# Clustered attention and SwiGLU on one core: q, k and x transposed off TensorE in the later part

## The chip, the core and the metric

The kernel runs on one core of a Trainium2 chip. A core has a matrix engine (TensorE, PE in the profile; its weight loads are PEld), VectorE (DVE), ScalarE (ACT), GpSimd (POOL), a queue engine that issues transfers (SyncE, SP) and 16 DMA engines. The engines run side by side, each through its own list of instructions in order, and wait for one another by semaphores. The metric is the time of one execution on the device, in microseconds (us); less is better.

## The reference

Inputs are float32: q, k, v of 4 batches x 8 heads x 768 tokens x 64, 16 centroids per head, and the weights of a feed-forward layer. The output is 3072 x 512 float32.

```python
def _attn_ref(q, k, v, centroids):              # q, k, v: (4, 8, 768, 64)
    ...
    q_assign = np.argmax(np.einsum('bhsd,hcd->bhsc', q_n, c_n), axis=-1)
    k_assign = np.argmax(np.einsum('bhsd,hcd->bhsc', k_n, c_n), axis=-1)
    mask = q_assign[:, :, :, None] == k_assign[:, :, None, :]
    scores = scale * np.matmul(q, k.transpose(0, 1, 3, 2))
    scores = np.where(mask, scores, -1000000000.0)
    ...                                         # softmax over the keys
    return np.matmul(attn, v)

def _moe_ref(x, w_gate, w_val, w_out, rms_g):   # x: (3072, 512), d_ff 1536
    rms = np.sqrt(np.mean(x * x, axis=-1, keepdims=True) + 1e-06)
    xn = x / rms * rms_g
    g = xn @ w_gate
    silu = g * (1.0 / (1.0 + np.exp(-g)))
    return silu * (xn @ w_val) @ w_out
```

A query attends only to the keys of its own cluster. The heads of a token, side by side, are the rows x of the second part.

## The kernel before

The work is cut in eight units (a batch, and half of its queries: 384 tokens by 8 heads; u = 0 to 7 in the code) and eight groups of four heads (g = 0 to 7), in which q and k are prepared. Head n of 32 belongs to group n // 4. While TensorE computes the scores of unit u, the gaps are filled with the second part for units u - 1 and u - 2, and from u = 1 on with the preparation of group u + 2 (and of group 2 in unit 1).

Loads come in rows of six tokens per partition, and TensorE transposes q and k, 128 columns at a time, into PSUM. ACT moves them to `qkT`; GpSimd and VectorE cast them to bf16 into `qext` and `kext`.

```python
    def src(a, n):
        b, h = divmod(n, H)
        return a[b, h].rearrange("(p t) d -> p t d", t=ST)      # ST = 6

    def load(n, part, on=None):
        if n not in staged:
            staged[n] = stage.tile([P, 2, ST, D], F32, tag="qk", name="qk")   # 6 buffers
        (on or nc.sync).dma_start(out=staged[n][:, part], in_=src((q, k)[part], n))
    ...
    def trans(g, h, part, on=None):
        if (g, h // 2) not in qkT:
            qkT[g, h // 2] = qk32.tile([P, 2, 2, UQ], F32, tag="qkT", name="qkT")
        qk = staged[g * HG + h]
        ps = ps_g.tile([P, UQ], F32, tag="gen", name="tq")
        for i in range(HT):                                     # HT = 3
            nc.tensor.transpose(ps[:, i * P:(i + 1) * P], qk[:, part, 2 * i:2 * i + 2].rearrange("p t d -> p (t d)"),
                                ident_f)
        to, by = qkT[g, h // 2][:, h % 2, part], 1.0 / ZS if part else 1.0
        if on is nc.vector:
            nc.vector.tensor_scalar_mul(to, ps, by)
        else:
            nc.scalar.activation(to, ps, ACT.Copy, scale=by)
```

The centroids are multiplied with `qkT` (tile `sc`). VectorE makes one-hot rows of the largest products and transposes them (`oh`); `place` writes them by DMA into rows 64 to 79 of `qext` and `kext`. A score of two tokens of the same cluster so has a large constant added, which the exponential takes away again.

```python
    def place(on, g, m, es=(0, 1)):
        ext = (kext if m else qext)[g % 4]
        for h in range(HG):
            for e in es:
                on.dma_start(out=ext[D:D + NC, h, e * UQ:(e + 1) * UQ],
                             in_=put[g, m][32 * h + e * NC:32 * h + (e + 1) * NC])
```

Group 2 is placed from SyncE, later ones from GpSimd. The attention writes x (`pv`). Its squares are summed by ACT (by VectorE for units 0 and 1), VectorE normalizes, TensorE transposes, and VectorE evicts with the gain of the norm:

```python
    def rms(u):
        x, nt = xs[u], UNITS[u][2]
        for t in range(nt):
            squares(u, t, True)
        ...                                                     # y = 1 / rms, nine small VectorE instructions
        for t in range(nt):
            nc.vector.tensor_scalar_mul(xn[u][:, t], x[:, t], y[:, t:t + 1])

    def xtrans(u, c):
        if c == 0:
            xnT[u] = xp.tile([P, CC, UQ], BF16, tag="xnT", name="xnT")
        ps = ps_g.tile([P, UQ], BF16, tag="gen", name="tx")
        w = UNITS[u][2] * P
        for t in range(UNITS[u][2]):
            nc.tensor.transpose(ps[:, t * P:(t + 1) * P], xn[u][:, t, c * P:(c + 1) * P], ident)
        nc.vector.tensor_scalar_mul(xnT[u][:, c, :w], ps[:, :w], gcol[:, c:c + 1])
```

`gv(u, f, val)` multiplies `xnT` with a block of 128 columns of a weight (four matmuls, tile `gate` or `val`); `out_mm(u, t, part)` does a third of an output row block (four matmuls, tile `o`). In `attention`, after each piece of scores (`s`: two matmuls and one exponential by ACT) fill is issued in proportion to its listed cost:

```python
    for u in range(1, NU):
        ...
            fill = ffn_work(u - 2)[CUT:] + [(0.0, lambda u=u: rms(u - 1))]
            fill += ... border(o, ffn)              # o pieces of unit u - 2, xtrans of unit u - 1 among the last
            attention([(u, h) for h in range(H)], fill + spread(ffn[CC:CUT], group(g) if g < NG else []), 1 if g < NG else 0)
```

So a unit holds, in this order, the last 8 gate or val pieces of unit u - 2, the norm of u - 1, the 9 output pieces of u - 2 with the transposes of x, and 16 gate or val pieces of u - 1 with the preparation of a group. Head n + 6 of q and k, and head n + 8 of v, are loaded as head n is prepared.

Of the kernel before, what the change touches and what calls it, by code (L numbers as in the profile page):

```python
# [9 lines left out]
F32 = mybir.dt.float32  # L10
BF16 = mybir.dt.bfloat16
# [11 lines left out]
def kernel(  # L23
# [27 lines left out]
    scale = 1.0 / (D ** 0.5)  # L51
    KR = D + NC
    WARM = 7
    CUT = CC + 2 * FC - 8
    LEAD = 6
    NQ, NV = 6, 8

    ctx.enter_context(tc.manual_schedule())
    pool = lambda n, b, **kw: ctx.enter_context(tc.tile_pool(name=n, bufs=b, **kw))
# [16 lines left out]
    def src(a, n):  # L76
        b, h = divmod(n, H)
        return a[b, h].rearrange("(p t) d -> p t d", t=ST)

    def load(n, part, on=None):  # L80
        if n not in staged:
            staged[n] = stage.tile([P, 2, ST, D], F32, tag="qk", name="qk")
        (on or nc.sync).dma_start(out=staged[n][:, part], in_=src((q, k)[part], n))

    def load_qk(n):
        if n < B * H:
# [6 lines left out]
        stagedv[n] = stage.tile([P, ST, D], F32, tag="vs", name="vs", bufs=NV)  # L93
        (vq or nc.sync).dma_start(out=stagedv[n], in_=src(v, n))

    c_in = const.tile([P, D], F32)
    nc.sync.dma_start(out=c_in, in_=centroids.rearrange("h c d -> (h c) d"))
    load(0, 0)
    load(0, 1, nc.scalar)
# [2 lines left out]
    for n in range(2, NQ):  # L102
        load(n, 1)
        load(n, 0)
    gcol = const.tile([P, CC], F32)


    qext = [const.tile([P, HG, S], BF16, name=f"qext{i}") for i in range(4)]
# [30 lines left out]
        return y2  # L139


    ones = const.tile([P, 32], F32)
    nc.vector.memset(ones, 1.0)
    cnt = const.tile([P, 32], F32)
    nc.vector.tensor_tensor_scan(cnt, ones, ones, 0.0, op0=ALU.mult, op1=ALU.add)
    cntT = const.tile([P, 32], F32)
    nc.vector.transpose(cntT, cnt)
    ident_f = const.tile([P, P], F32)
    nc.vector.memset(ident_f, 0.0)
# [13 lines left out]

    cblk = const.tile([P, H, 2 * NC], F32)
    nc.gpsimd.memset(cblk, 0.0)
    c_sq = const.tile([P, D], F32)
# [9 lines left out]
    c_n = const.tile([P, 2 * D], F32)  # L176
    nc.vector.tensor_scalar_mul(c_n[:, :D], c_in, c_inv)
    nc.vector.tensor_scalar_mul(c_n[:, D:], c_in, c_inv)

# [22 lines left out]
    def trans(g, h, part, on=None):  # L202
        if (g, h // 2) not in qkT:
            qkT[g, h // 2] = qk32.tile([P, 2, 2, UQ], F32, tag="qkT", name="qkT")
        qk = staged[g * HG + h]
        ps = ps_g.tile([P, UQ], F32, tag="gen", name="tq")
        for i in range(HT):
            nc.tensor.transpose(ps[:, i * P:(i + 1) * P], qk[:, part, 2 * i:2 * i + 2].rearrange("p t d -> p (t d)"),  # L208
# [11 lines left out]
    def cast(on, g, h, part, es=(0, 1)):  # L220
        for e in es:
            to = cols((kext if part else qext)[g % 4][:D, h], g, e)
            of = qkT[g, h // 2][e * D:(e + 1) * D, h % 2, part]
            if on is nc.scalar:
                nc.scalar.copy(to, of)
            else:
                on.tensor_copy(to, of)  # L227
# [138 lines left out]
    def squares(u, t, last):  # L366
        if (t, last) == (0, False):
            sq[u] = small.tile([P, 2, HT], F32, tag="ss", name="ss")
            xn[u] = xp.tile([P, HT, DM], BF16, tag="xn", name="xn")
        c = slice(DM - 2 * D, DM) if last else slice(0, DM - 2 * D)  # L370
        to = sq[u][:, int(last), t:t + 1]
        if u <= 1:
            nc.vector.scalar_tensor_tensor(xn[u][:, t, c], xs[u][:, t, c], 1.0 / DM, xs[u][:, t, c], op0=ALU.mult,
                                           op1=ALU.mult, accum_out=to)
        else:
            nc.scalar.activation(xn[u][:, t, c], xs[u][:, t, c], ACT.Square, scale=DM ** -0.5, accum_out=to)  # L376
# [5 lines that stand above are left out]
        ms = small.tile([P, HT], F32, tag="ms", name="ms")  # L382
        nc.vector.scalar_tensor_tensor(ms[:, :nt], sq[u][:, 0, :nt], 1e-6, sq[u][:, 1, :nt], op0=ALU.add, op1=ALU.add)
        y = rsqrt(ms[:, :nt], nt)
        for t in range(nt):
            nc.vector.tensor_scalar_mul(xn[u][:, t], x[:, t], y[:, t:t + 1])

    xnT, gvT = {}, {}

# [4 lines that stand above are left out]
        w = UNITS[u][2] * P  # L394
        for t in range(UNITS[u][2]):
            nc.tensor.transpose(ps[:, t * P:(t + 1) * P], xn[u][:, t, c * P:(c + 1) * P], ident)  # L396
        nc.vector.tensor_scalar_mul(xnT[u][:, c, :w], ps[:, :w], gcol[:, c:c + 1])  # L397

    def xtrans_all(u):

        xnT[u] = xp.tile([P, CC, UQ], BF16, tag="xnT", name="xnT")
        ps = [ps_g.tile([P, 2, UQ], BF16, tag="gen", name="tx") for _ in range(3)]
        to = [ps[(c + 1) // 2][:, (c + 1) % 2] for c in range(CC)]
        for t in range(HT):
            for c in range(CC):
                nc.tensor.transpose(to[c][:, t * P:(t + 1) * P], xn[u][:, t, c * P:(c + 1) * P], ident)
        for c in range(CC):
            if c < CC - 1:
                nc.vector.tensor_scalar_mul(xnT[u][:, c], to[c], gcol[:, c:c + 1])
            else:  # L410
                nc.scalar.activation(xnT[u][:, c], to[c], ACT.Copy, scale=gcol[:, c:c + 1])

    gates = {}

# [53 lines left out]
    def group_work(g):  # L468

        t, c = [], []  # L470
        for h in range(HG):
            n = g * HG + h
            t += [(0.3, lambda h=h: trans(g, h, 0)), (0.3, lambda h=h: trans(g, h, 1))]

            def others(n=n):
                vcast(n)
                load_qk(n + NQ)
                load_v(n + NV)

            def both(h=h, f=others):  # L480
                cast(nc.gpsimd, g, h, 0)
                f()
                cast(nc.vector, g, h, 1, (0,))
            if g == 2:
                c.append((0.0, others))
            else:
                c += [(0.0, both), (0.0, lambda h=h: cast(nc.vector, g, h, 1, (1,)))]
# [15 lines left out]
        return [x for pair in zip(t, c) for x in pair] + c[len(t):]  # L503

    def group(g):
        t, c, a = group_work(g)
        return [x for h in range(HG) for x in t[2 * h:2 * h + 2] + c[2 * h:2 * h + 2]] + a

    def spread(a, b):

# [9 lines left out]

    def ffn_work(u):
        n = UNITS[u][2] / HT
        w = [(0.18 * n, lambda c=c: xtrans(u, c)) for c in range(CC)]
        for f in range(FC):
            for val in (False, True):
                w.append((0.64 * n, lambda f=f, val=val: gv(u, f, val)))
        return w
# [4 lines left out]
    def border(o, ffn):  # L532

        return o[:-2] + ffn[:2] + o[-2:-1] + ffn[2:4] + o[-1:]


    def tokens(g, h, on=None):
# [28 lines left out]
        load_v(n)  # L566
    for n in range(H, H + HG):
        load_qk(n)
    nc.sync.dma_start(out=gcol, in_=moe_rms_g.rearrange("(c p) -> p c", p=P), allow_slow_non_contiguous=True)
    tokens(0, 2)  # L570
    casts(pool_, 2, K0, K1, Q0)
    pair_clusters(0, (1,))
# [84 lines left out]
    for u in range(1, NU):  # L657
        ffn, o, g = ffn_work(u - 1), out_work(u - 2) if u > 1 else [], u + 2
        if u == 1:
# [16 lines left out]
            fill = spread(ffn[CC:CUT], prep)  # L676
# [9 lines left out]
        f()  # L686
    rms(NU - 1)
    nc.scalar.activation(first_exp, off, ACT.Silu)
    for _, f in border(out_work(NU - 2), ffn_work(NU - 1)) + ffn_work(NU - 1)[CC:] + out_work(NU - 1)[:-3]:
        f()  # L690
    for i in range(3):
        out_part(NU - 1, HT - 1, i)
# [30 lines left out]
```

The softmax here doesn't subtract the row's maximum and nothing guards it: scores larger than these inputs give would overflow.

## Time and profile before

The median of three executions is 345.5 us (345.27 to 345.8); the profiled one spans 343.6 us. The clock that TensorE was granted is full throughout.

| engine | busy us | instructions |
|---|---|---|
| PE (matmuls and transposes) | 336.0 | 3045 |
| ACT | 259.7 | 449 |
| DVE | 219.9 | 540 |
| PEld (weight loads, beside PE) | 208.2 | 3045 |
| POOL | 112.9 | 225 |

The DMA engines are full in the first 77 us, when the weights come in too, and mostly idle later: 28.35 MB are read and 6.29 MB written in all, in 27,302 packets. A load of q or k is 192 KB and lands 3.9 us after its issue (median).

The page lists busy times first, then the chain of work that ended last, followed back from the last instruction: its shares say which engine the end of the program waited for. Groups by line give, for each line of the kernel, engine and tile, the busy time, the mean of one instruction in ns, the idle time of the engine before these instructions, and who ended it. A line reads `line engine operation out<-in`. TensorE overlaps its matmuls, so the duration of one is longer than the time it adds; the chain shows the latter.

### The profile page before, as it was taken

How to read it: one execution, taken by the hardware profiler on the slowest of the kernel's cores; microseconds unless marked ns; L12 is line 12 of the kernel's file. 1: busy time of each engine (PE TensorE's matmuls, PEld its weight loads, DVE VectorE, ACT ScalarE, POOL GpSimd, SP SyncE). 2: the span in 40 equal slices, each digit the busy share in tenths (PEclk: the TensorE clock that was granted, in tenths of full speed). 3: DMA queues.
4: the chain of work that ended last, by engine and by line, in shares of the span. 5: the costliest groups of instructions: out<-in, count | busy, mean ns of one | idle time of the engine just before them, and what ended most of it. 6: DMA issues, size and time to landing. Idle time of an engine off the chain costs nothing.

```text
span 343.6 us, 8003 instructions
## 1 busy us (share of the span) xinstructions
PE 336.0 (98%) x3045; PEld 208.2 (61%) x3045; DVE 219.9 (64%) x540; ACT 259.7 (76%) x449; POOL 112.9 (33%) x225
## 2 busy tenths in 40 slices
PE   8999999999999999999999999999999999999996
PEld 3547657555766567665675656756566656655654
DVE  6999796975577626785367745686455635575330
ACT  5899979856979768786797777888688877763322
POOL 6999596234335305271131801516000000000000
PEclk9999999999999999999999999999999999999999
DMA  8999989882450015401130011000100011001002
GB/s 276 384 210 216 248 166 237 134 267 97 149 158 14 31 62 152 139 18 40 61 94 2 23 53 41 2 5 21 63 32 0 2 46 49 2 1 64 31 2 92
DMA packets 27302, 31.62 MB, mean 92 GB/s; under 512 B 4480, under 2 KB 24320, under 8 KB 27264
## 3 DMA queue, kind: packets, MB, share of 16 engines
q1 hardware_dynamic: 18608, 25.02, 22.2%
q0 software_dynamic: 8368, 5.71, 10.4%
q8 instruction: 24, 0.39, 0.5%
q10 hardware_dynamic: 288, 0.39, 0.4%
q14 instruction: 14, 0.11, 0.1%
HBM read 28.35 MB, written 6.29 MB: 101 GB/s over the span
## 4 chain that ended last, share of the span: by engine, by line
PE 82%; ACT 9%; DVE 6%; DMA 1%; issue 1%; DVEq 0%; ACTq 0%
PE o L448 17%; PE val L423 16%; PE gate L423 16%; PE s L333 15%; PE acc L351 9%; ACT pT L337 6%; PE tq L208 4%; PE sc L241 3%; PE tx L396 1%; ACT xn L376 1%; ACT th L431 1%; DVE pads L312 1%; DVE kext L317 1%; DVE qext L317 1%; DMA c_in<-in_centroids_dram 1%
## 5 line engine op out<-in xcount | busy, mean ns | idle before, releaser
L337 ACT ACTIVATE pT<-s,off 128x768 bf16<-128x768 f32 x192 | 171.3, 905 | 39.7 <-PE s L333 38.7
L333 PE MATMUL s<-qext,kext 80*128 80x384 bf16 x384 | 94.8, 327 | 2.4 <-ACT pT L337 1.6
L432 DVE SCALAR_TENSOR_TENSOR th<-th,gate 128x384 f32<-128x384 f32 x84 | 46.4, 552 | 50.8 <-ACT th L431 50.6
L423 PE MATMUL gate<-xnT,wg 128*128 128x384 bf16 x384 | 78.5, 325 | 0.1
L423 PE MATMUL val<-xnT,wv 128*128 128x384 bf16 x384 | 78.1, 326 | 0.1
L448 PE MATMUL o<-wo,gvT 128*128 128x512 bf16 x276 | 67.6, 379 | 0.0
L227 POOL CAST qext<-qkT 64x384 bf16<-64x384 f32 x64 | 35.3, 558 | 72.3 <-ACT qkT L214 63.8
L333 PEld LDWEIGHTS <-kext 80*128 80x128 bf16 x384 | 36.4, 98 | 35.1 <-issue 9.9
L436 DVE SCALAR_TENSOR_TENSOR gvT<-th,val 128x384 bf16<-128x384 f32 x84 | 46.3, 551 | 6.8 <-PE val L423 2.0
L423 PEld LDWEIGHTS <-wv 128*128 128x128 bf16 x384 | 36.3, 97 | 22.4 <-issue 0.7
L423 PEld LDWEIGHTS <-wg 128*128 128x128 bf16 x384 | 36.2, 97 | 22.0 <-issue 0.8
L351 PEld LDWEIGHTS <-pT 128*128 128x128 bf16 x1152 | 43.4, 97 | 10.1 <-DVE x L358 1.0
L431 ACT ACTIVATE th<-gate 128x384 f32<-128x384 f32 x84 | 41.3, 492 | 9.4 <-PE gate L423 8.8
L351 PE MATMUL acc<-vbf,pT 128*128 128x65 bf16 x1152 | 45.7, 193 | 0.6 <-ACT pT L337 0.2
L448 PEld LDWEIGHTS <-gvT 128*128 128x128 bf16 x276 | 25.6, 97 | 25.2 <-issue 0.6
L208 PE MATMUL tq<-ident_f,qk 128*128 128x128 f32 x192 | 30.9, 276 | 0.0
L282 POOL DMA_DIRECT2D qext<-oh x40 | 19.1, 486 | 34.7 <-DVE oh L271 28.3
L214 ACT ACTIVATE qkT<-tq 128x384 f32<-128x384 f32 x57 | 27.4, 494 | 3.4 <-PE tq L208 2.9
L397 DVE TENSOR_SCALAR xnT<-tx,gcol 128x384 bf16<-128x384 bf16 x28 | 10.4, 412 | 27.5 <-PE tx L396 27.5
L208 PEld LDWEIGHTS tq<-ident_f,qk 128*128 128x128 f32 x192 | 23.2, 141 | 6.6 <-ACT qkT L214 1.0
L451 ACT COPY o_sb<-o 128x512 f32<-128x512 f32 x23 | 13.5, 586 | 15.5 <-PE o L448 15.5
L282 POOL DMA_DIRECT2D kext<-oh x40 | 19.1, 485 | 9.6 <-DVE oh L271 9.6
(81 smaller groups left out, 246.2 us busy)
## 6 DMA issues: line engine op xcount, KB each, us to landing
qk<-in_q_dram SPq DMA_DIRECT2D x32, 192.0 KB, 3.9
vs<-in_v_dram SPq DMA_DIRECT2D x32, 192.0 KB, 4.2
out_dram<-o_sb SPq DMA_DIRECT2D x23, 256.0 KB, 2.0
qk<-in_k_dram SPq DMA_DIRECT2D x30, 192.0 KB, 3.9
wg<-in_moe_w_gate_dram POOLq DMA_DIRECT2D x4, 384.0 KB, 8.7
wv<-in_moe_w_val_dram POOLq DMA_DIRECT2D x4, 384.0 KB, 11.0
wo<-in_moe_w_out_dram POOLq DMA_DIRECT2D x3, 512.0 KB, 8.9
qext<-oh POOLq DMA_DIRECT2D x40, 12.0 KB, 1.6
```

The source lines that it names most:

```text
L208: nc.tensor.transpose(ps[:, i * P:(i + 1) * P], qk[:, part, 2 * i:2 * i + 2].rearrange("p t d -> p (t d)"), ident_f)
L214: nc.scalar.activation(to, ps, ACT.Copy, scale=by)
L227: on.tensor_copy(to, of)
L282: on.dma_start(out=ext[D:D + NC, h, e * UQ:(e + 1) * UQ], in_=put[g, m][32 * h + e * NC:32 * h + (e + 1) * NC])
L333: nc.tensor.matmul(ps[:, j, :w] if nt == HT else flat[:, j * w:(j + 1) * w], lhsT=cols(kext[g % 4][:KR, hh], g, kc // HT, kc % HT * P, (kc ...
L337: nc.scalar.activation(pT[u, h][:, n * i:n * i + n, :w], of, ACT.Exp, bias=off, scale=scale * ZS)
L351: nc.tensor.matmul(acc[:, h % 2, t], lhsT=pT[u, h][:, kc, t * P:(t + 1) * P], rhs=vbf[g % 4][:, hh, kc % HT * 2 + kc // HT], start=kc == 0 ...
L423: nc.tensor.matmul(ps, lhsT=w[:, c, f * P:(f + 1) * P], rhs=xnT[u][:, c, :n], start=c == 0, stop=c == CC - 1)
L431: nc.scalar.activation(th, ps, ACT.Tanh, scale=0.5)
L432: nc.vector.scalar_tensor_tensor(th, th, 1.0, ps, op0=ALU.add, op1=ALU.mult)
L436: nc.vector.scalar_tensor_tensor(gvT[u][:, f, :n], gates[u], 0.5, ps, op0=ALU.mult, op1=ALU.mult)
L448: nc.tensor.matmul(outs[u], lhsT=gvT[u][:, f, t * P:(t + 1) * P], rhs=wo[:, f], start=f == 0, stop=f == FC - 1)
```

## The change

It takes two kinds of transposes from TensorE.

First, q and k of heads 16 to 31 (from the fifth group on). Their loads bring in half rows of 32 numbers (128 bytes) and put them so that a transpose within blocks of 32 x 32 gives the same layout as a full one: the 32 partitions of a block hold 32 tokens, and the four blocks of partitions are the two halves of the tokens by the two halves of a row. VectorE then does the transpose straight into `qkT`, between output pieces, and nothing passes through PSUM or ACT. The scaling of k moves into its cast, and the casts of k go from VectorE to GpSimd.

Second, x of the second to the seventh unit is transposed by a DMA from SyncE, as soon as it is normalized. For this the gain of the norm is multiplied in by the normalizing instruction, as a row, where it was a column at the eviction. The first and the last unit stay with TensorE.

The order of the fill changes with it: the block transposes and the casts stand among the output pieces, the work on clusters among the gate and val pieces. The squares of the second unit move from VectorE to ACT. A few small constants of the start share a buffer, to make room.

```diff
     def load(n, part, on=None):
         if n not in staged:
             staged[n] = stage.tile([P, 2, ST, D], F32, tag="qk", name="qk")
-        (on or nc.sync).dma_start(out=staged[n][:, part], in_=src((q, k)[part], n))
+        if n < BG * HG:                                         # BG = 4, HG = 4
+            (on or nc.sync).dma_start(out=staged[n][:, part], in_=src((q, k)[part], n))
+            return
+
+        to = staged[n][:, part].rearrange("p t d -> p (t d)").rearrange("p (i r d) -> p i r d", i=HT, d=32)
+        of = (q, k)[part][n // H, n % H].rearrange("(r p i e) (c d) -> e c p i r d", p=32, i=HT, e=2, d=32)
+        for e in range(2):
+            for c in range(2):
+                r = 32 * (2 * e + c)
+                nc.sync.dma_start(out=to[r:r + 32], in_=of[e, c])
...
@@ trans
         qk = staged[g * HG + h]
+        if g >= BG:
+            nc.vector.transpose(qkT[g, h // 2][:, h % 2, part], qk[:, part].rearrange("p t d -> p (t d)"))
+            return
...
@@ cast
-            if on is nc.scalar:
+            if part and g >= BG:
+                on.tensor_scalar_mul(to, of, 1.0 / ZS)
+            elif on is nc.scalar:
...
@@ squares
-        if u <= 1:
+        if u == 0:
...
@@ rms
         for t in range(nt):
-            nc.vector.tensor_scalar_mul(xn[u][:, t], x[:, t], y[:, t:t + 1])
+            nc.vector.scalar_tensor_tensor(xn[u][:, t], x[:, t], y[:, t:t + 1], grow, op0=ALU.mult, op1=ALU.mult)
+        if 0 < u < NU - 1:
+            xnT[u] = xp.tile([P, CC, UQ], BF16, tag="xnT", name="xnT")
+            for t in range(nt):
+                nc.sync.dma_start_transpose(out=xnT[u][:, :, t * P:(t + 1) * P], in_=xn[u][:, t])
...
@@ group_work
-                cast(nc.vector, g, h, 1, (0,))
+                cast(nc.gpsimd if g >= BG else nc.vector, g, h, 1, (0,))
...
@@ the loop over units, u >= 2
             fill = ffn_work(u - 2)[CUT:] + [(0.0, lambda u=u: rms(u - 1))]
-            fill += border(spread(o[:3], [(0.0, f) for _, f in a3[5:]]) + o[3:], ffn) if u == 2 else border(o, ffn)
-            attention([(u, h) for h in range(H)], fill + spread(ffn[CC:CUT], group(g) if g < NG else []), 1 if g < NG else 0)
+            rows, clusters = group(g)                           # transposes and casts; cluster work
+            if u == 2:
+                fill += spread(o[:3], [(0.0, f) for _, f in a3[5:]])
+                o = o[3:]
+            fill += spread(o, rows) + spread(ffn[:CUT], clusters)
+            attention([(u, h) for h in range(H)], fill, 1 if g < NG else 0)
```

More of the change, by code (lines that the diff above doesn't have):

```diff
@@ L53 @@
     WARM = 7
-    CUT = CC + 2 * FC - 8
+    CUT = 2 * FC - 8
     LEAD = 6
     NQ, NV = 6, 8
+    BG = 4
     ctx.enter_context(tc.manual_schedule())
@@ L94, in load_v @@
         (vq or nc.sync).dma_start(out=stagedv[n], in_=src(v, n))
-    c_in = const.tile([P, D], F32)
+    boot = gate.tile([P, UQ], F32, tag="th", name="boot")
+    c_in, c_sq, c_n = boot[:, :D], boot[:, D:2 * D], boot[:, 2 * D:4 * D]
+    ones, cnt, cntT = [boot[:, 4 * D + 32 * i:4 * D + 32 * i + 32] for i in range(3)]
     nc.sync.dma_start(out=c_in, in_=centroids.rearrange("h c d -> (h c) d"))
@@ L104 @@
         load(n, 0)
-    gcol = const.tile([P, CC], F32)
+    grow = const.tile([P, DM], F32)
     qext = [const.tile([P, HG, S], BF16, name=f"qext{i}") for i in range(4)]
@@ L139, in rsqrt @@
         return y2
-    ones = const.tile([P, 32], F32)
     nc.vector.memset(ones, 1.0)
-    cnt = const.tile([P, 32], F32)
     nc.vector.tensor_tensor_scan(cnt, ones, ones, 0.0, op0=ALU.mult, op1=ALU.add)
-    cntT = const.tile([P, 32], F32)
     nc.vector.transpose(cntT, cnt)
@@ L165 @@
     nc.gpsimd.memset(cblk, 0.0)
-    c_sq = const.tile([P, D], F32)
     c_ss = const.tile([P, 1], F32)
@@ L175 @@
     nc.vector.reciprocal(c_inv, c_norm)
-    c_n = const.tile([P, 2 * D], F32)
     nc.vector.tensor_scalar_mul(c_n[:, :D], c_in, c_inv)
@@ L396, in xtrans @@
             nc.tensor.transpose(ps[:, t * P:(t + 1) * P], xn[u][:, t, c * P:(c + 1) * P], ident)
-        nc.vector.tensor_scalar_mul(xnT[u][:, c, :w], ps[:, :w], gcol[:, c:c + 1])
+        nc.vector.tensor_copy(xnT[u][:, c, :w], ps[:, :w])
     def xtrans_all(u):
@@ L408, in xtrans_all @@
             if c < CC - 1:
-                nc.vector.tensor_scalar_mul(xnT[u][:, c], to[c], gcol[:, c:c + 1])
+                nc.vector.tensor_copy(xnT[u][:, c], to[c])
             else:
-                nc.scalar.activation(xnT[u][:, c], to[c], ACT.Copy, scale=gcol[:, c:c + 1])
+                nc.scalar.copy(xnT[u][:, c], to[c])
     gates = {}
@@ L472, in group_work @@
             n = g * HG + h
-            t += [(0.3, lambda h=h: trans(g, h, 0)), (0.3, lambda h=h: trans(g, h, 1))]
+            w = 0.0 if g >= BG else 0.3
+            t += [(w, lambda h=h: trans(g, h, 0)), (w, lambda h=h: trans(g, h, 1))]
             def others(n=n):
@@ L486, in group_work @@
             else:
-                c += [(0.0, both), (0.0, lambda h=h: cast(nc.vector, g, h, 1, (1,)))]
+                c += [(0.0, both), (0.0, lambda h=h: cast(nc.gpsimd if g >= BG else nc.vector, g, h, 1, (1,)))]
         a = []
@@ L505, in group @@
     def group(g):
+        if g >= NG:
+            return [], []
         t, c, a = group_work(g)
-        return [x for h in range(HG) for x in t[2 * h:2 * h + 2] + c[2 * h:2 * h + 2]] + a
+        return [x for h in range(HG) for x in t[2 * h:2 * h + 2] + c[2 * h:2 * h + 2]], a
     def spread(a, b):
@@ L522, in ffn_work, with border @@
         n = UNITS[u][2] / HT
[L523 to L527, printed above, removed]
+        return [(0.64 * n, lambda f=f, val=val: gv(u, f, val)) for f in range(FC) for val in (False, True)]
     def out_work(u):
         return [(0.86, lambda t=t, p=p: out_mm(u, t, p)) for t in range(UNITS[u][2]) for p in range(3)]
-    def border(o, ffn):
-        return o[:-2] + ffn[:2] + o[-2:-1] + ffn[2:4] + o[-1:]
+    def border(o, u):
+        x = [(0.18, lambda c=c: xtrans(u, c)) for c in range(CC)]
+        return o[:-2] + x[:2] + o[-2:-1] + x[2:] + o[-1:]
     def tokens(g, h, on=None):
@@ L568 @@
         load_qk(n)
-    nc.sync.dma_start(out=gcol, in_=moe_rms_g.rearrange("(c p) -> p c", p=P), allow_slow_non_contiguous=True)
+    nc.sync.dma_start(out=grow, in_=moe_rms_g.unsqueeze(0).broadcast_to([P, DM]))
     tokens(0, 2)
@@ L675 @@
             hooks[1, *divmod(LEAD - 1, HT)] = lambda: xtrans_all(0)
-            fill = spread(ffn[CC:CUT], prep)
+            fill = spread(ffn[:CUT], prep)
             attention([(1, h) for h in range(H)], fill, LEAD, hooks)
@@ L688 @@
     nc.scalar.activation(first_exp, off, ACT.Silu)
-    for _, f in border(out_work(NU - 2), ffn_work(NU - 1)) + ffn_work(NU - 1)[CC:] + out_work(NU - 1)[:-3]:
+    for _, f in border(out_work(NU - 2), NU - 1) + ffn_work(NU - 1) + out_work(NU - 1)[:-3]:
         f()
```

## The prediction

> **What bounds the kernel now.** I began with part 1 of the page, the busy time of each engine.
>
> ```profile
> PE 336.0 (98%) x3045; PEld 208.2 (61%) x3045; DVE 219.9 (64%) x540; ACT 259.7 (76%) x449; POOL 112.9 (33%) x225
> ```
>
> TensorE is busy all the time, but its matmuls overlap, so 98% does not prove that it is the bound. Part 4, the chain that ended last, does:
>
> ```profile
> PE 82%; ACT 9%; DVE 6%; DMA 1%; issue 1%; DVEq 0%; ACTq 0%
> ```
>
> Then I asked for the chain between 130 and 190 us, a whole steady unit (its ACT pieces come at 103.06, 144.08 and 185.11 us, so a unit lasts 41.0 us). Columns: start, length, what.
>
> ```profile
> 165.26 0.34 PE tx L396 x6
> 165.59 0.86 PE o L448 x4
> ...
> 168.31 0.65 PE gate L423 x4
> 168.97 0.33 PE tq L208 x3
> 169.29 0.33 PE s L333 x2
> 169.62 0.55 PE acc L351 x18
> ...
> 183.16 1.43 PE sc L241 x16
> ```
>
> The pieces stand end to end, so each takes its whole length from the time. Three fp32 transposes of q or k (tq) cost 0.33 us, six bf16 ones of x (tx) 0.34 us; the 276 and 219 ns that the groups by line give are latencies that overlap. A sum checks the bound. A unit has 24 pieces of s (0.33), 8 acc (0.55), 24 gate or val (0.65), 9 o (0.865), tx (0.68), 8 tq (2.64), sc (1.43): 7.9 + 4.4 + 15.6 + 7.8 + 0.7 + 2.6 + 1.4 = 40.4 of 41.0 us. The other 0.6 us lies mostly where the chain passes through ACT at the unit's end, as squares fall on top of exponentials there.
>
> The groups by line give what the moved work costs:
>
> ```profile
> L214 ACT ACTIVATE qkT<-tq 128x384 f32<-128x384 f32 x57 | 27.4, 494 | 3.4 <-PE tq L208 2.9
> L227 DVE CAST kext<-qkT 64x384 bf16<-64x384 f32 x42 | 15.6, 371 | 1.8 <-ACT qkT L214 0.7 <-POOL vbf L230 0.2
> L227 POOL CAST kext<-qkT 64x384 bf16<-64x384 f32 x22 | 13.6, 617 | 2.9 <-DVE qkT L212 2.1
> L317 DVE STREAM_TRANSPOSE kext<-pads 32x384 int32<-32x384 int32 x8 | 4.6, 572 | 0.5
> ```
>
> Last I looked at SyncE's queue, which issues nearly all loads in one order (timeline, 44 to 76 us). It matters because the change multiplies its instructions.
>
> ```profile
> 52.90 0.37 SPq L94 DMA_DIRECT2D vs<-in_v_dram  x1
> 53.48 3.24 SPq L282 DMA_DIRECT2D qext<-oh  x4
> 56.82 7.75 SPq L282 DMA_DIRECT2D kext<-oh  x8
> 64.61 4.35 SPq L282 DMA_DIRECT2D qext<-oh  x4
> 69.21 0.37 SPq L83 DMA_DIRECT2D qk<-in_q_dram  x1
> ```
>
> The queue never rests here: four loads, sixteen placing transfers of group 2 in 15.5 us, then twelve loads to 75 us, one each 0.46 us. Unit 2 starts at about 65.3 us, and its first scores need the kext pieces issued from 56.8 us on, which take 6.4 us to land. The slack is a microsecond or two.
>
> **What the Trainium skill says.** "TensorE: Matmul & The Clock Gate", Part 4: PE-mode transpose, gives about 275 ns for a 128x128 transpose inside a kernel. The trace agrees on the duration (276 ns), but on the chain only 110 ns of each can be won. "VectorE: DVE Perf Modes", The three transpose paths, has VectorE transpose within 32x32 blocks only, which is why the load must now lay out blocks, and puts a DMA transpose of 128x128 at 1309 ns; "Advanced Engine Details and Errata", X-Bar Transpose (TRN2), calls transposing DMAs as fast as regular ones. No run here has one yet. "DMA: Bandwidth & Descriptors", Why small descriptors are slow (HBM only), puts a fixed cost on each packet. The trace's nearest are a group's 16 placing transfers (12 KB each, 384-byte packets, 512 in all): in the window 148.3 to 158.0 us, with little else, the DMA share is 0.08, and 0.08 x 9.7 us x 16 engines / 512 is 24 ns a packet.
>
> **The change, part by part.**
>
> TensorE. Groups 4 to 7 lose 16 heads x 2 tensors = 32 pieces of 0.33 us, 10.6 us. Units 1 to 6 lose 0.68 us of tx each, 4.1 us. Nothing is added. All lies on the chain: 14.7 us.
>
> ACT loses 32 evictions of 494 ns, 15.8 us, and takes the squares of unit 1, 3 x (527 + 298 + 2 x 198 ns) = 3.7 us. A steady unit: 24 exponentials x 0.905 + 12 tanh x 0.492 + squares 3.7 + 3 output copies x 0.586 = 33.1 us. TensorE will need 40.4 - 2.6 - 0.7 = 37.1 us, so ACT stays below it, and with less backlog at a unit's end I give back 1 us over all units.
>
> VectorE gains 32 block transposes of 572 ns, 18.3 us. It loses 24 evictions of x (412 ns, 9.9 us), 32 casts of k (371 ns, 11.9 us) and unit 1's squares (3 x (602 + 288 + 2 x 81) = 3.2 us). The normalizing multiplies by a second tensor: from the squares' two shapes, 602 ns at 384 columns and 288 at 128, I estimate 760 ns at 512, against 483, which over 24 is 6.6 us. Sum: about zero. In the built program the transposes stand between the output pieces, where no gate or val is evicted.
>
> GpSimd gets 32 casts more, at the 617 ns of its present ones 19.7 us, 4.9 us in each of four units where it now has 6.1 us of casts and 7.6 us of issuing. It fits.
>
> SyncE and DMA. Each of 32 loads becomes four issues and 1536 packets of 128 bytes, where it was 128 of 1536. A head has 192 packets on each engine: at 24 ns 4.6 us, or 19 us for the four heads of a 37 us unit, loaded a unit and a half ahead. In steady units 32 issues for q and k, 4 for v, 3 outputs and 3 transposes at 0.46 us take 19 us. That is hidden. The start is not. In SyncE's order between 50.17 us (where the load of head 16 starts now) and the first transposing DMA stand 18 issues (heads 16, 17 and two of v; 6 now), the 16 placing transfers, then 36 issues (heads 18 to 21 and four of v; 12 now). At 0.46 to 0.65 us, as the engines are full there (DMA share 0.92 to 1.15 from 52 to 64 us) and each waits for the one eight before, that is 50.2 + 8.3 to 11.7 + 15.5 + 36 x 0.47 = 91 to 94 us. The placing starts 5 to 8 us late, so unit 2's first scores wait 3 to 6 us. And the three transposes of unit 1's x are issued at 91 to 94 us and land some 3 to 4 us later, at 96: its first gate, now at 86.26 us, would be ready for it at about 86. Both waits overlap, so unit 2 pays some 10 us, once.
>
> The DMA transpose in later units. VectorE writes the xn of the unit shown from 160.09 to 161.4 us. After the change the last comes at about 162.3, and the first gate would start at 167.5: 5 us for three transposes of 128 KB. A load of 192 KB lands 3.9 us after issue, an output of 256 KB after 2.0. That just fits; I allow 0.3 us a unit, 1.7 in all.
>
> Sum: 345.5 - 14.7 - 1 + 10 + 1.7 = 341.5. Since the 10 us take SyncE's slow pace over the whole stretch, I put the time a little under it: 340.5 us.
>
> **Rivals.** (a) The queue's jam is hidden. For: at 0.46 us an issue and 0.6 for each placing, without waits, the transposes go out at 50.2 + 8.3 + 9.6 + 16.6 = 84.7 us and land near 88, so that 2 us are lost and the time is 333. Against: the placing shows 0.97 us a transfer now, with fewer packets in the engines.
>
> (b) The DMA transposes are slow in every unit. For: a kind of transfer without a trace, 5 us of slack. Against: they are issued when the queue is empty (DMA share 0.01 to 0.1 late in the kernel). If three take 2 us more, five later units pay 10 us: 350. If all twelve 128x128 blocks of a unit followed one another at 1309 ns, 15.7 us, units would pay 10 us each: near 390.
>
> (c) The small packets bound the loads. The page's hardware queue takes 0.222 x 16 x 343.6 us for 18,608 packets, 65.6 ns each. At that, a head needs 12.6 us and four heads 50, more than a unit; VectorE would stand waiting for q and k with the evictions behind it: 360 or more. Against: those packets average 1344 bytes, and the 24 ns of 384-byte ones is the better guide.
>
> (d) ACT binds at the units' ends: some 1 us per unit, 6 us more.
>
> **Range and chances.** The saving on TensorE is well measured; what is open is what makes it wait. Waits of less than 9 us in all leave it under 338.6 (faster by over 2%): 0.36. Waits of 9 to 22 us keep it within 2%: 0.47. More, by (b) or (c): 0.17. The range, from 3 to 22 us of waits, is 332 to 352.
>
> **What would show it.** tq must be gone from the chain after unit 1, tx from units 1 to 6, and units 3 to 5 must repeat every 37.5 us. Unit 2 must be longer, with scores waiting for DMA into kext and the first gate for DMA into xnT at 95 us. If (b) holds, every unit's first gate waits so. If (c), VectorE's transposes wait for qk, with a DMA share near full from 50 to 200 us. If (d), s waits for pT. I am wrong if unit 2 shows no such wait, or if steady units stay at 41 us.

## The result, and the profile after

The changed kernel takes 357.0 us (median of four runs, 354.8 to 357.5), the kernel before beside it 345.65 us: a ratio of 1.032, with a 95% interval of 1.029 to 1.035. It is slower, by 11.4 us. The prediction was 340.5 us.

First two lines of the changed kernel's page: busy times, and the chain's shares by engine.

```profile
PE 325.3 (91%) x2877; PEld 194.3 (55%) x2877; DVE 222.6 (63%) x504; ACT 248.0 (70%) x429; POOL 150.3 (42%) x257
...
PE 71%; DVE 10%; SPq 6%; ACT 5%; DMA 3%; issue 3%; POOL 1%; ACTq 0%; DVEq 0%; POOLq 0%
```

TensorE has the 168 instructions less that were to go, and 10.7 us less of busy time. But 9% of the span is now idle on it, where it was 2%, and SyncE's queue (SPq) carries 6% of the chain, where it did not appear before. The mean granted clock is 0.966, where it was 1. The changed kernel's table of waits names what TensorE stood for (engine, line, what was waited for, then us in total, times, longest):

```profile
PE gate L439 <- DMA xnT<-xn: 12.4, 1, 12.4
PE s L345 <- DMA kext<-oh: 8.9, 1, 8.9
```

Each is one single wait, and both lie in unit 2. The changed kernel's chain from 74 to 115 us shows where; columns are start, length, what:

```profile
74.66 1.44 PE s L345 x4
76.10 0.99 PE acc L363 x18
77.09 1.28 PE gate L439 x4
78.37 1.28 PE val L439 x4
...
80.21 0.65 PE gate L439 x4
...
108.44 2.44 DMA xnT<-xn
111.02 1.44 PE gate L439 x4
112.45 1.28 PE val L439 x4
113.73 0.59 PE s L345 x2
```

The first scores of unit 2 start at 74.66 us, after 8.9 us for `kext`; the first gate at 111.02 us, after 12.4 us for `xnT`. After each wait the pieces are slow for a while. The four from 74.66 us take 1.44 + 0.99 + 1.28 + 1.28 = 4.99 us, where they would take 0.66 + 0.55 + 0.65 + 0.65 = 2.51: 2.5 us lost. At 80.21 us a gate is back at 0.65. The three from 111.02 us take 3.31 instead of 1.63: 1.7 us. The clock granted is 0.69 around the first wait, 0.60 from 98 to 111 us, and full again from 115 us on (table by windows of the changed kernel: window, its length, busy times of PE, PEld, DVE, ACT, POOL, then PEclk, DMA share, GB/s):

```profile
66.00:76.00 10.00, 1.34 (x6) 0.64 (x7) 1.40 (x3) 1.23 (x4) 3.87 (x8) 0.69 0.52 94
```

What released the second wait is SyncE's queue. Here is its timeline in the changed kernel from the load of head 16 on (start, length, line, what, how many):

```profile
51.46 3.30 SPq L93 DMA_DIRECT2D qk<-in_q_dram  x4
...
63.32 6.18 SPq L93 DMA_DIRECT2D qk<-in_k_dram  x4
69.61 0.57 SPq L104 DMA_DIRECT2D vs<-in_v_dram  x1
70.28 2.47 SPq L294 DMA_DIRECT2D qext<-oh  x4
72.84 4.96 SPq L294 DMA_DIRECT2D kext<-oh  x8
...
80.43 2.64 SPq L93 DMA_DIRECT2D qk<-in_q_dram  x4
...
104.97 0.56 SPq L104 DMA_DIRECT2D vs<-in_v_dram  x1
105.71 3.94 SPq L402 DMA_TRANSPOSE xnT<-xn  x3
```

The queue issues without a pause from 51 to 110 us. The 18 issues ahead of the placing take 18.8 us (51.46 to 70.28), the placing 10.1, the 36 issues behind it 25.2 (80.43 to 105.6). Most of the small issues take 0.62 us, but nine of the sixteen ahead of the placing take 0.85 to 2.00 us. Seven of the nine lie after 56 us, and from 56 to 68 us the DMA share is 1.16 to 1.22 (table by windows). From 80 to 105 us, where it is 0.49, one of 32 is so long. Only then do the transposes go out, though VectorE had finished `xn` at 90.8 us by the chain.

The rest is as hoped. The ACT pieces that mark the units' ends come at 125.84, 163.43 and 201.01 us: 37.6 us for a unit, where it was 41.0. The mark at the end of unit 2 comes 22.8 us later than before (103.06), although the unit has 3.4 us less to do: some 26 us went there, 0.8 of them before it began (the last scores of unit 1 start at 64.58 us, before at 63.81).

The balance: 345.65 - 14.7 (transposes gone from TensorE) + 8.9 + 12.4 (waits) + 2.5 + 1.7 (slow clock after them) = 356.5 us; measured 357.0.

### The profile page after: what moved, and what is told of

It reads as the page before. It is cut to its first block, busy times and chain, and to the rows that moved or that the text cites. A ratio compares the mean times of both kernels' runs of the same rounds, so it can differ in the third digit from the quotient of the medians.

```text
span 355.6 us, 7858 instructions
## 1 busy us (share of the span) xinstructions
PE 325.3 (91%) x2877; PEld 194.3 (55%) x2877; DVE 222.6 (63%) x504; ACT 248.0 (70%) x429; POOL 150.3 (42%) x257
## 4 chain that ended last, share of the span: by engine, by line
PE 71%; DVE 10%; SPq 6%; ACT 5%; DMA 3%; issue 3%; POOL 1%; ACTq 0%; DVEq 0%; POOLq 0%
PE gate L439 16%; PE val L439 16%; PE o L464 15%; PE s L345 14%; PE acc L363 8%; SPq L93 4%; ACT pT L349 2%; PE sc L253 2%; ACT xn L388 1%; DVE xn L398 1%; ACT th L447 1%; POOL kext L294 1%; DVE kext L329 1%; DVE qext L329 1%; DVE pads L324 1%
## 5 line engine op out<-in xcount | busy, mean ns | idle before, releaser
L345 PE MATMUL s<-qext,kext 80*128 80x384 bf16 x384 | 95.9, 331 | 11.3 <-DMA kext<-oh 8.9
L439 PE MATMUL gate<-xnT,wg 128*128 128x384 bf16 x384 | 79.6, 330 | 12.5 <-DMA xnT<-xn 12.4
L439 PE MATMUL val<-xnT,wv 128*128 128x384 bf16 x384 | 79.5, 330 | 0.0
L235 POOL TENSOR_SCALAR kext<-qkT 64x384 bf16<-64x384 f32 x32 | 37.3, 1165 | 1.3
L368 DVE RECIPROCAL inv<-acc 128x6 f32<-128x6 f32 x32 | 6.0, 188 | 33.1 <-PE acc L363 32.6
L467 ACT COPY o_sb<-o 128x512 f32<-128x512 f32 x23 | 13.5, 586 | 15.8 <-PE o L464 15.8
L370 DVE TENSOR_TENSOR x<-acc,inv 128x384 f32<-128x384 f32 x32 | 17.8, 557 | 1.1
L388 ACT ACTIVATE xn<-x 128x384 bf16<-128x384 f32 (+1 forms) x42 | 17.3, 415 | 0.0
```

What stands on the lines that cost most here:

```text
L235: on.tensor_scalar_mul(to, of, 1.0 / ZS)
L345: nc.tensor.matmul(ps[:, j, :w] if nt == HT else flat[:, j * w:(j + 1) * w], lhsT=cols(kext[g % 4][:KR, hh], g, kc // HT, kc % HT * P, (kc ...
L439: nc.tensor.matmul(ps, lhsT=w[:, c, f * P:(f + 1) * P], rhs=xnT[u][:, c, :n], start=c == 0, stop=c == CC - 1)
```

## The experiments

The trace offers more than one reading, and the expectations name them by letter. **A**: SyncE's queue is the cause. It works in order, the many small issues take longer each than was assumed, and whatever stands behind them comes late, in unit 2 and nowhere else. **B**: the transposing DMA is slow or late in itself. **D**: the two waits are independent losses, so that taking one away gives all of it back. **E**: a small issue is slow because of its short packets, and not because there are four for one. All edits are to the changed kernel unless another is named; the kernel before ran beside each at 345.6 to 345.8 us.

### Only x by DMA

q and k are loaded and transposed as before; the rest of the change stays.

```diff
-    BG = 4
+    BG = 8
```

> The changed kernel with q and k loaded and transposed as before in all groups; only x of units 1 to 6 goes by DMA. Theory A (SyncE's queue is too long in unit 2, because of the small loads): the queue reaches unit 1's transposes near 78 us, no gate waits for xnT for more than a microsecond, and the time is 345.6 - 4.1 + up to 1 = 341.5 to 342.5 us. Rival B (the DMA transpose is itself slow): the first gate of every unit waits, and the time is 345 us or more.

341.45 us (341.29 to 341.61), ratio 0.987 [0.986, 0.989]. No wait for `xnT` is left; in the queue's timeline the same three transposes go out 26 us earlier:

```profile
79.26 3.91 SPq L402 DMA_TRANSPOSE xnT<-xn  x3
```

The six units' tx, 4.1 us, are saved in full (345.8 - 4.1 = 341.7). The transposing DMA costs nothing when the queue ahead of it is short, so B falls, and so does the prediction's rival (b).

### Only q and k in half rows

x of units 1 to 6 goes through TensorE again, between the last two output pieces.

```diff
-        if 0 < u < NU - 1:
+        if False:
...
+            x = [(0.18, lambda c=c, u=u: xtrans(u - 1, c)) for c in range(CC)]   # set among the last two o pieces
```

> The changed kernel with x of all units transposed by TensorE; only q and k of heads 16 to 31 go by small loads and VectorE. Theory A: the scores of unit 2 still wait some 9 us for kext, with some 2.5 us of slow clock behind it, and nothing waits for xnT: 345.6 - 10.6 + 9 + 2.5 = 346.5, 345 to 349 us. Rival C (the 128-byte packets fill the DMA engines through the kernel, and VectorE stands waiting for q and k in every unit): 355 us or more. Rival B: without the DMA transposes nothing is lost, under 338 us.

344.96 us (343.82 to 346.87), 0.998 [0.996, 0.999], at the lower end of what was expected. In the table of waits the one for the placed rows stands alone:

```profile
PE s L345 <- DMA kext<-oh: 7.7, 2, 7.4
```

The tq pieces give 10.6 us, the waits take 7.7, and the clock after them most of what is left: this part alone is nearly a null. By themselves the two parts measure -4.3 and -0.8 us, together -5.1, and the change, which has both, +11.4. What costs it is their meeting in one queue.

### x of unit 1 through TensorE

```diff
-        if 0 < u < NU - 1:
+        if 1 < u < NU - 1:
...  # xtrans(1, c) among the last two o pieces of unit 2
```

> The changed kernel with x of unit 1 alone transposed by TensorE, x of units 2 to 6 by DMA. Theory A: the wait of 12.4 us for xnT and the slow clock behind it (1.2 us) go, 0.7 us of tx comes back, the wait for kext stays: 357 - 12.9 = 344 us (342 to 346). Rival B: the other five units go on waiting, and at most 3 us are won.

342.91 us (341.37 to 343.7), 0.991 [0.988, 0.994]. So 14.1 us (357.04 - 342.91) hang on whether the x of one unit stands in that queue. The waits of this run:

```profile
PE s L345 <- DMA kext<-oh: 7.3, 1, 7.3
PE gate L439 <- DMA xnT<-xn: 0.9, 1, 0.9
```

The 0.9 us is already in unit 3, where unit 2's transposes leave at 129.7 us: the queue has not caught up by then.

### Placing first

The loads of heads 16 and 17 (and of two of v) are issued behind the placing of group 2 instead of ahead of it.

```diff
             def others(n=n):
                 vcast(n)
-                load_qk(n + NQ)
-                load_v(n + NV)
+                if n not in (10, 11):
+                    load_qk(n + NQ)
+                    load_v(n + NV)
...
-                (place(nc.sync, g, 1), place(nc.sync, g, 0, (1,)))
+                (place(nc.sync, g, 1), place(nc.sync, g, 0, (1,)),
+                 [(load_qk(i + NQ), load_v(i + NV)) for i in (10, 11)])
```

> The changed kernel with the loads of heads 16 and 17 issued after the placing of group 2, not ahead of it. Theory A: the wait of 8.9 us for kext goes, but the queue holds as many issues ahead of unit 1's transposes as it did, so the first gate still starts at 107 to 111 us after a wait of some 20 us for xnT, and the time stays at 352 to 357 us. Rival D (two separate losses, which add up): 357 - 8.9 - 2.5 = 345.5 us.

353.78 us (353.52 to 354.79), 1.024 [1.022, 1.026]. The first wait shrinks from 8.9 to 0.4 us, and the second grows from 12.4 to 18.1 (table of waits):

```profile
PE gate L439 <- DMA xnT<-xn: 18.1, 1, 18.1
```

D fell: taking the first wait away gave 3.3 us, not the 11 that it and its slow clock take in the trace. It had hidden part of the second. What sets the time is when the transposes leave (105.71 us in the change, 101.15 here). The 18 issues of heads 16 and 17 that took 18.8 us ahead of the placing take 13.3 behind it (62.98 to 76.33). The waits and their clock don't quite account for this run: 345.8 - 14.7 + 18.5 + some 1.8 is 351.4, and 2.4 us stay unexplained.

### Both

```diff
-        if 0 < u < NU - 1:
+        if 1 < u < NU - 1:
...  # and the placing first, as above
```

> The changed kernel with both relocations: heads 16 and 17 loaded after the placing of group 2, and x of unit 1 transposed by TensorE. Theory A: neither kext nor xnT is waited for in unit 2; VectorE waits a few us for heads 18 and 19, whose loads are issued only by 88 us. 345.8 - 14.7 + 0.7 + 2 to 5 = 334 to 337 us. Rival D (the losses are separate): 353.8 - 14 = 340. If the slow clock or the small packets cost something of their own in every unit, 340 or more.

342.85 us (340.44 to 343.3), 0.989 [0.984, 0.993]: a miss by 6 to 9 us. Unit 2 is clean, and the same wait, 7.8 us, has moved to unit 3, where the first gate starts at 135.1 us. The transposes of unit 2 in the queue's timeline:

```profile
129.78 3.95 SPq L402 DMA_TRANSPOSE xnT<-xn  x3
```

I had taken the jam as over after unit 2, and that part of A fell. By my estimate a steady unit's queue has 36 issues at 0.66 us, three transposes at 1.3 and three outputs at some 0.4, or 29 us of 37.6: it can make up 8 us in a unit, and the jam is longer than that. By 160 us it has caught up: it issues nothing from 160.5 us until unit 3's transposes at 166.59.

### Heads 16 to 19 as before

```diff
-    BG = 4
+    BG = 5
```

> The changed kernel with the new loads from group 5 on, not from group 4 (one number). Theory A: the queue ahead of unit 1's transposes holds 18 slow issues (heads 20, 21 and two of v) where it held 54, and the placing of group 2 is where it was before the change. No wait for kext; the transposes go out near 85 us, so the gate waits 3 to 5 us. Saving 14.7 - 2.7 = 12.0; 345.8 - 12.0 + 4 = 338 us (335 to 340).

334.36 us (333.79 to 338.01), 0.969 [0.963, 0.975]: faster than both kernels, with one number changed, and a little under the range expected. It keeps x by DMA in all six units. It gives back 8 tq (2.6 us), and takes 24 issues out of the very stretch that jams; the transposes leave at 87.5 us. The profiled execution, at 338.0 the longest of the four, still waits for `kext`:

```profile
PE s L345 <- DMA kext<-oh: 2.1, 1, 2.1
```

After it the clock is halved for 3.4 us (70.03 to 73.44), which costs 1.7. These 3.8 us are what sets it apart from the other three (333.8 to 334.9).

### The kernel before, its loads in four

Here the kernel before loads heads 16 to 31 with four issues for one, each of 32 partitions with whole rows of 1536 bytes. Nothing else changes, and there are no short packets.

```diff
# kernel before
-        (on or nc.sync).dma_start(out=staged[n][:, part], in_=src((q, k)[part], n))
+        if n < 16:
+            (on or nc.sync).dma_start(out=staged[n][:, part], in_=src((q, k)[part], n))
+            return
+        for r in range(0, P, 32):
+            nc.sync.dma_start(out=staged[n][r:r + 32, part], in_=src((q, k)[part], n)[r:r + 32])
```

> The kernel before, with each load of q and k of heads 16 to 31 split in four issues of 32 partitions, in rows of 1536 bytes as before: four times the issues without small packets. What does an issue cost? Theory E (an issue costs 0.33 to 0.46 us whatever it carries; the 0.66 us of the small loads come from their 384 packets): these issues take 0.33 to 0.46 us. Rival F (a load of 32 partitions costs more to issue, whatever its packets): 0.62 us and more. With E the queue is done with head 21 near 85 us and nothing waits but perhaps the first scores of unit 2 for kext (up to 3 us): 345.5 to 349 us. With F: 350 or more.

353.19 us (two runs, 352.6 and 353.77), 1.021 [1.017, 1.025]: slower than I expected. The count of issues by itself pushes the placing back from 53.48 to 61.76 us, which costs a wait of 4.6 us for `kext` and a slow stretch after it. The window around it (columns as above), and four issues of a load in the queue's timeline:

```profile
65.00:75.00 10.00, 5.44 (x37) 3.04 (x36) 4.22 (x11) 2.89 (x5) 3.86 (x8) 0.66 0.40 79
```

```profile
89.40 1.82 SPq L87 DMA_DIRECT2D qk<-in_k_dram  x4
```

The wait and the slow pieces after it (s 1.42, acc 0.99, gate 1.28, val 0.95: 2.1 us more than at full clock) are 6.7 of the 7.5 us lost. On the length of an issue E holds so far: four for one, and 32 partitions, aren't what makes it long, since 1.82 us for four is 0.45 each, where the change has 0.66. Whether it is the shortness of the runs, their number or their layout isn't separated: a placing transfer has only 16 rows of 768 bytes and takes 0.51 to 0.59 us. The same 18 issues ahead of the placing take 11.1 us here (50.61 to 61.7) and 18.8 in the change, the 36 behind it 18.3 (73.37 to 91.7) and 25.2.

### Placing first, and heads 20 and 21 behind the transposes

```diff
-                    load_qk(n + NQ)
+                    if n not in (14, 15):
+                        load_qk(n + NQ)
...
             if u == 2:
+                fill += [(0.0, lambda: (load_qk(20), load_qk(21)))]     # after the norm of unit 1
```

> As with the placing first, and the loads of heads 20 and 21 (16 issues) moved behind unit 1's transposing DMAs, which are kept. Theory A: the transposes go out 16 x 0.66 = 10.6 us earlier, at 90.5 us, the wait for xnT shrinks from 18 to some 7.5 us, and the time falls by as much: 353.8 - 10.6 = 343 us (341 to 346). If something else than the number of issues ahead of them delays the transposes, 350 us or more.

347.9 us (20 runs, 344.7 to 350.59), 1.005 [1.003, 1.007]: above the range. The transposes left when expected, at 91.11 us, and the first gate waited 8.7 us for them; but the moved issues then met those of unit 2, and 2.7 us of waiting came in unit 3. The table of waits adds both up:

```profile
PE gate L439 <- DMA xnT<-xn: 11.4, 2, 8.7
```

With these waits the sum is 345.6 - 14.7 + 11.4 = 342.3. The clock is halved after both of them, also after the second, which was only 2.7 us long (chain, columns as above):

```profile
136.75 2.46 DMA xnT<-xn
...
139.35 1.44 PE gate L439 x4
140.79 1.28 PE val L439 x4
```

The work done at half clock, 5.3 and 3.3 us, costs half of that, 4.3 us: 346.6. The profiled execution took 348.8, and I can't place the other 2.2 us. Reordering passes the delay on. The queue's work must become less, or what hangs on it must.

### Both, and unit 2's x through TensorE as well

Only x of units 3 to 6 goes by DMA, once the queue has caught up; all of q and k from head 16 on stay in half rows.

```diff
-        if 0 < u < NU - 1:
+        if 2 < u < NU - 1:
...  # xtrans for units 1 and 2; the placing first
```

> As with both relocations, and x of unit 2 transposed by TensorE too, so that only units 3 to 6 use the DMA. Theory A (SyncE's backlog wandered from unit 2 into unit 3, where the transposes left at 129.8 us): the wait of 7.8 us there and its slow clock (1.7 us) go, 0.7 us of tx comes back, and no other wait takes its place, because by 160 us the queue has caught up. 342.9 - 8.8 = 334 us (332.5 to 336). If the backlog wanders on into unit 4, or VectorE waits for q and k instead, 338 or more.

333.26 us (331.78 to 334.02), 0.964 [0.962, 0.966]: the fastest kernel here, 12.5 us under the one before. TensorE waits for DMA only once, for 0.4 us, and the clock is full throughout. Its busy times:

```profile
PE 321.2 (97%) x2886; PEld 193.9 (59%) x2901; DVE 225.1 (68%) x512; ACT 248.1 (75%) x429; POOL 151.2 (46%) x257
```

345.7 - 14.7 + 1.4 (two units' tx back) is 332.4. So the saving on TensorE that the prediction counted is real, to within 0.9 us, once the queue's delay is out of the way. The 1 us more that it gave back for ACT doesn't show.

### Heads 16 to 19 as before, with the placing first

```diff
-    BG = 4
+    BG = 5
...  # the placing first
```

> New loads from group 5 on, and heads 16 and 17 loaded after the placing of group 2. Theory A: the wait for kext that the run with group 5 still shows (2.1 us and its slow clock, in some executions) goes; the transposes of unit 1 leave as late as before (87 us), so 0 to 3 us of wait for xnT may come instead. 332.5 to 334.5 us, against 334.4.

334.12 us (333.96 to 334.47), 0.967 [0.966, 0.968]. No wait of TensorE for DMA, and the runs lie closer together than without the placing first (334.36). By the sum, with 8 tq left on TensorE, it is 345.7 - 14.7 + 2.6 = 333.6.

### The same, with unit 1's x through TensorE

```diff
-    BG = 4
+    BG = 5
-        if 0 < u < NU - 1:
+        if 1 < u < NU - 1:
...  # the placing first
```

> The same, and x of unit 1 transposed by TensorE. Theory A: nothing of unit 2 waits for SyncE any more; 0.7 us of tx more. 345.6 - 14.7 + 2.7 + 0.7 = 334.3; 333 to 335 us. If waits for xnT remained in the run before it, this one is the faster.

336.52 us (336.48 to 336.86), 0.974 [0.973, 0.975]: a miss. It costs 2.4 us over the run above and should cost 0.7. Unit 2 is longer, with TensorE less busy from 66 to 104 us (36.69 of 38 us here, 37.45 there), and no wait on DMA stands in that stretch. The table of waits has another one there, at 86.4 us:

```profile
PE tx L412 <- ACT qkT L224: 0.7, 1, 0.7
```

The tiles `tx` and `tq` share buffers in PSUM (tag `gen`), and in this variant TensorE still transposes q and k of group 4 in unit 2: the first tx stands until ACT has emptied a tq. With 0.26 us of standing before an sc at 94.5 us and the 0.68 of tx itself this is 1.7 of the 2.4 us; the rest stays open.

### Heads 16 to 19 as before, k casts left to VectorE

```diff
-    BG = 4
+    BG = 5
-                cast(nc.gpsimd if g >= BG else nc.vector, g, h, 1, (0,))     # both halves
+                cast(nc.vector, g, h, 1, (0,))
```

> New loads from group 5 on, and all casts of k left on VectorE (0.37 us each), where GpSimd takes 1.165 us. Theory A: the casts lie beside TensorE's work, so it makes no difference: within 1 us of the run with group 5, 333.5 to 335.5 us. If GpSimd's slower casts hold up the placing of a group and with it the next unit, this one is faster by more.

336.63 us (336.39 to 337.8), 0.974 [0.973, 0.975]: 2.3 us slower than with the casts on GpSimd, where I expected no difference. The cluster products wait for VectorE, their matmuls 1.7 us and the weight loads ahead of them 4.0 (table of waits):

```profile
PEld sc L253 <- DVE th L448: 4.0, 4, 1.3
```

With the casts on GpSimd (heads 16 to 19 as before) the latter is 1.0 us and the former absent. So moving the casts is worth some 0.8 us (2.3 over three groups) in each unit that prepares such a group (units 3 to 5 repeat every 38.3 us, with the casts on GpSimd every 37.6), although a cast takes 459 ns on VectorE and 1166 on GpSimd. VectorE's sum of busy time (69% of the span here, 66% with the casts on GpSimd) didn't show this.

## Why the prediction was wrong

**The step that failed** is SyncE's pace at the start: "At 0.46 to 0.65 us ... that is 50.2 + 8.3 to 11.7 + 15.5 + 36 x 0.47 = 91 to 94 us." The transposes left at 105.71 us. Term by term: a start 1.3 us later; 18.8 us for the 8.3 to 11.7; 10.1 for the 15.5 of the placing (in the kernel before, SyncE stood 4.7 of these waiting for earlier transfers, which it doesn't here); 25.2 for the 17. The issue cost came from issues of 1536-byte rows. The kernel before with its loads in four issues has just that case, and there the two terms are 11.1 and 18.3 us, near the prediction; even the wait of its first scores is 4.6 us, inside the 3 to 6. So the count was right, and what was mis-sized is the time of an issue of 128-byte runs, in two ways. Behind the placing it is 0.66 us with what lies between two, where 0.47 was taken. Ahead of it, where up to 0.65 was allowed, 18 issues at 0.66 would be 12 us; most of the other 7 is in the nine long ones. They stand where the DMA engines are fullest, and the same loads moved behind the placing take 13.3 us. That full engines draw the small issues out fits both, but that they do isn't shown by a run made for it. The transposes then take 5.2 us to land instead of 3 to 4, so the landing is at 110.9 instead of "at 96", and the end moved with it.

"Both waits overlap, so unit 2 pays some 10 us, once" was right in kind: it pays once, in unit 2, in the two places that the prediction named, and the later wait sets the total, as the run with the placing first shows. But it pays 25.5 us: 8.9 + 12.4, and 4.2 of slow clock. With 25.5 in place of 10 the prediction's sum is 341.5 + 15.5 = 357.0, which is what was measured. That it fits so closely is luck: the sum still holds 1 us won on ACT and 1.7 us of waits in later units, and the runs show neither. The slow clock, 4.2 us in all, I hadn't thought of; "TensorE: Matmul & The Clock Gate", What's actually happening, in the Trainium skill, says that TensorE falls to half its clock after an idle window of about 3.4 us and needs about as long at work to recover. On the half clock the trace agrees: after 8.9 us of waiting the pieces take nearly twice their time for 5.0 us, after 12.4 us for 3.3. On the length of the wait the runs decide otherwise: 2.7 us (heads 20 and 21 moved) and 2.1 us (heads 16 to 19 as before) were enough, each with 3.4 us of half clock after it.

**What held.** tq and tx left the chain where they should, 14.7 us, which the fastest variant confirms within 0.9 us. Steady units repeat every 37.6 us (37.5 predicted). ACT is busy 248.0 us: 259.7 - 15.8 + 3.7 was 247.6. VectorE's sum moved by 2.7 us ("about zero"), with the normalizing multiply at 748 ns (760) and the block transpose at 542 (572).

**The rivals.** (a), the jam hidden: refuted, the transposes leave at 105.7 us and not at 84.7. (b), slow transposes in every unit: refuted by the run with x alone, and by the absence of any such wait after unit 2; the twelve blocks of a unit have landed 5.2 us after the first issue, not 15.7. (c), small packets binding the loads: refuted, as VectorE's transposes never wait for them by the table of waits. The changed kernel's hardware queue on the page (packets, MB, share of 16 engines):

```profile
q1 hardware_dynamic: 74608, 27.64, 31.6%
```

Before it was 18,608 packets and 22.2%. So 56,000 more packets cost 0.316 x 16 x 355.6 - 0.222 x 16 x 343.6 = 577 us of engine time, net. They are of several kinds: 49,152 of 128 bytes for q and k stand in place of 4,096 of 1536, and some 9,200 of 256 bytes come with the transposing DMAs. The packet records have 13.0 ns for the mean one of 128 bytes. The 24 ns was a misreading: the 512 packets of that window are not of 384 bytes, but 256 of 768 bytes (36.6 ns) and 256 of 4 (9 ns). (d), ACT at the units' ends: no scores wait for pT longer than 0.3 us at a time.

**Off the path,** one more size was wrong: the k casts on GpSimd multiply as well, and take 1165 ns, not 617, 37.3 us for 19.7. No chain shows them as the cause here.

**What stays open:** what in an issue of 384 short runs takes the 0.2 us more than one of 32 long rows, and up to 1.4 us more ahead of the placing (the trace has the length only); some 2 us of the run with the placing first, and as much where heads 20 and 21 are moved as well; 0.7 us of unit 1's x in the variant with heads 16 to 19 as before.

## What to carry to other kernels

Before a load is split, count the issues on its queue between now and the next transfer that something waits for, and multiply by an issue time measured on transfers of that shape; bytes alone don't give it, and where the engines are full it was longer still. A transfer newly put on a crowded in-order queue inherits the whole backlog: bring it in once the queue has drained, or split less where it is full. A backlog drains only with what a unit leaves of its own length (here some 8 of 37.6 us, estimated), so a wait that is cured in one unit may come up in the next.

## What the runs showed of the hardware that was not expected

- A SyncE issue mostly takes 0.33 to 0.43 us for a whole load (128 rows of 1536 bytes), 0.42 for a quarter of it in whole rows (32 rows; 0.45 with what lies between two), and 0.62 for a quarter in 384 runs of 128 bytes (0.66). The last is the same at 99 us, amid the jam (2.58 us for four), and at 183.7 us (2.59), shortly after a DMA share of 0.01. So these 0.62 us are not a wait for busy DMA engines. A long one is likeliest where the engines are fullest: of the 1280 small issues in the changed kernel and ten of its variants 86 took more than 0.8 us, 14 of the 23 with a DMA share over 1.2 in the 2 us before, and 72 of the other 1257.
- The length isn't the issue's own alone. A whole load of v, right behind small loads, takes longer too (same variant, heads 16 to 19 as before; first behind whole loads, then behind small ones):

```profile
72.66 0.38 SPq L104 DMA_DIRECT2D vs<-in_v_dram  x1
...
80.00 0.55 SPq L104 DMA_DIRECT2D vs<-in_v_dram  x1
```

- Short packets are cheap in the engines: 13.0 ns of one engine for 128 bytes, against 65.6 ns for the mean packet of the kernel before. By the byte they cost more.
- A transposing DMA of 128 x 512 bf16 takes 1.2 to 1.3 us to issue and lands 2.4 us after; three in a row are 3.9 us of the queue.
- A wait of TensorE of 2.1 us, with 0.4 us of standing shortly before it, was enough to bring the slow clock (1.7 us lost after it); after 4.6 us 2.1 were lost, after 12.4 us 1.7. By the clock records of the eight kernels with such waits the half-clock stretches last 3.4, 6.8, 10.2, 13.7 or 17.1 us, the waiting in them included.
